# Key blocks of a decode attention dealt to the partitions in another order

One Trainium2 chip, one core. The metric is the device time of one execution in microseconds (us); lower is better. Ratios between two kernels are the mean time of one kernel's fast runs over that of the other's fast runs of the same rounds, so they are not quite the ratio of the medians quoted beside them.

## The reference

One decode step: layer norm of 4 rows of 512, then attention over a cache and a small gated feed-forward in parallel, summed with x. What matters here is the size of the cache, 4 batches x 32 heads x 8192 keys x 128 in bf16, for K and for V:

```python
q = ((xn @ wq).reshape(B, 1, 32, 128)).transpose(0, 2, 1, 3)
scores = einsum("bhqd,bhkd->bhqk", q, k_cache) * 128 ** -0.5
p = softmax(scores)                          # over 8192 keys
o = einsum("bhqk,bhkd->bhqd", p, v_cache)    # any order of keys gives the same sum
return x + o.transpose(...).reshape(B, 1, 4096) @ wo + swiglu_ffn(xn)
```

That is 256 blocks (128 of K, 128 of V) of 2 MiB, each read once: 536.9 MB of the 550.8 MB that the kernel reads.

## The kernel before

Each (head, batch) pair is one step. Its K block goes to one of nine slots of 128 partitions x 16 KiB, V four steps behind. The row of a partition is 64 keys in a row in HBM, 16 KiB. DVE, the vector engine, transposes K; PE, the matrix engine, makes scores and, for V, the weighted sum. Partitions are the 128 rows of SBUF, the memory on the chip; HBM is the large memory beside it. The profile shows 16 DMA engines that carry data between the two in packets: 33330 of the 42210 packets are of 8 KB or more, here mostly one row of 16 KiB each.

```python
T = Sk // P                # 64 keys for each partition
SLOT = T * Dh              # 8192 bf16 = 16 KiB for each partition
NSLOT = 9
...
def load_k(m):
    h, b = divmod(m, B)
    t_ = slot()
    nc.sync.dma_start(out=t_[:], in_=A_k_cache[b, h, :, :].rearrange("(p t) d -> p (t d)", p=P))
    k_tiles[m] = t_

def load_v(m, parts=1):
    h, b = divmod(m, B)
    t_ = slot()
    src = A_v_cache[b, h, :, :].rearrange("(p t) d -> p (t d)", p=P)
    w = SLOT // parts
    for i in range(parts):
        nc.sync.dma_start(out=t_[:, i * w:(i + 1) * w], in_=src[:, i * w:(i + 1) * w])
    v_tiles[m] = t_
...   # (cut: layer norm, q projection, feed-forward, softmax, output projection)
for i in range(M + LP + 1):          # M = 128 steps, LP = 4
    if i + 2 < M:
        load_k(i + 2)
    if 0 <= i + 2 - LP < M:
        load_v(i + 2 - LP, parts=4 if i + 2 - LP == M - 1 else 1)
    ...   # output weights are loaded at steps 115 and 116 as rows of 1 KiB
```

## Time and profile before

| | before |
|---|---|
| median of 4 runs | 1310.61 us (1310.52 to 1310.66) |
| DMA rate over the span | 421 GB/s |
| DMA engines busy | 99.5% of the span |
| PE / DVE busy | 1089.7 / 693.8 us |

The DMA engines bound the kernel; the prediction shows the lines. Two more lines of the page are needed for comparison. The first is the rate of the DMA in 40 equal slices of the span, the second the transfers of K (count, size, median us from issue to landing):

```profile
GB/s 393 429 425 428 426 427 428 427 427 426 427 429 426 426 428 426 427 428 425 429 426 428 426 427 427 427 426 427 428 428 426 425 429 426 427 394 412 425 428 288
slot<-in_A_k_cache_dram SPq DMA_DIRECT2D x128, 2048.0 KB, 39.0
```

The rate is flat at about 427 GB/s; the dip to 394 is where the output weights pass.

### The profile page before, as it was taken

The numbers are of one execution on the slowest core, as the hardware profiler recorded it, in microseconds if no ns is written. First come the engines' busy times: TensorE is split into PE (matmuls) and PEld (weight loads), VectorE is DVE, ScalarE is ACT, GpSimd is POOL, SyncE is SP. The second block draws the span as 40 slices with busy tenths as digits, with TensorE's granted clock in tenths as the row PEclk, the third lists the DMA queues.
The fourth block names the chain that finished last, engine by engine and source line by source line (L and its number), as shares of the span: only waits on it lengthen the run. The fifth ranks groups of instructions, "written<-read, shape, count | busy, mean of one in ns | idle before, by whom it ended". The sixth has DMA issues, their size and how long they took to land.

```text
span 1308.9 us, 11179 instructions
## 1 busy us (share of the span) xinstructions
PE 1089.7 (83%) x4610; PEld 423.3 (32%) x4676; DVE 693.8 (53%) x887; ACT 48.6 (4%) x102; POOL 5.6 (0%) x11
## 2 busy tenths in 40 slices
PE   5888888888888888888888888888988888886887
PEld 2243333333333333333333333333333333332333
DVE  7634554554554564554565555455555555544542
ACT  1000000000000000000000000000000000000000
POOL 1000000000000000000000000000000000000000
PEclk8889999999999999999999899999999999997999
DMA  9999999999999999999999999999999999999996
GB/s 393 429 425 428 426 427 428 427 427 426 427 429 426 426 428 426 427 428 425 429 426 428 426 427 427 427 426 427 428 428 426 425 429 426 427 394 412 425 428 288
DMA packets 42210, 551.49 MB, mean 421 GB/s; under 512 B 4264, under 2 KB 8368, under 8 KB 8880
## 3 DMA queue, kind: packets, MB, share of 16 engines
q1 hardware_dynamic: 42160, 550.79, 99.5%
q8 instruction: 36, 0.59, 0.2%
q14 instruction: 14, 0.11, 0.0%
HBM read 550.77 MB, written 0.00 MB: 421 GB/s over the span
## 4 chain that ended last, share of the span: by engine, by line
DMA 91%; PE 5%; DVE 3%; issue 0%; SPq 0%; ACT 0%; DVEq 0%; ACTq 0%
DMA slot<-in_A_k_cache_dram 86%; DMA slot<-in_B_w_up_dram 3%; DMA slot<-in_A_v_cache_dram 3%; DVE kt L252 2%; PE oacc L72 2%; PE sps L72 2%; PE xps L72 0%; SPq L93 0%; PE mps L274 0%; SPq L85 0%; DVE mx L268 0%; DVE res L384 0%; DVE zq L243 0%; PE mps L72 0%; ACT o_sb L309 0%
## 5 line engine op out<-in xcount | busy, mean ns | idle before, releaser
L252 DVE STREAM_TRANSPOSE kt<-slot 128x1024 uint32<-128x1024 uint32 x512 | 593.6, 1212 | 300.1 <-DMA slot<-in_A_k_cache_dram 295.4
L72 PE MATMUL sps<-kt,zq 128*128 128x512 bf16 x1982 | 566.9, 415 | 196.7 <-DVE kt L252 176.4
L72 PEld LDWEIGHTS <-zq 128*128 128x128 bf16 x2048 | 208.9, 103 | 544.4 <-issue 375.9
L298 DVE RECIPROCAL rcp<-mps 128x4 f32<-128x4 f32 x32 | 5.8, 182 | 162.5 <-PE mps L72 162.5
L268 DVE TENSOR_REDUCE mx<-sps 128x1 f32<-128x512 f32 x32 | 22.1, 691 | 40.5 <-PE sps L72 40.5
L277 DVE TENSOR_REDUCE nm<-mps 128x4 f32<-128x64 f32 x32 | 7.2, 224 | 50.2 <-PE mps L274 50.2
L72 PE MATMUL xps<-ident_f,o_sb 128*128 128x4 f32 x256 | 33.1, 253 | 0.7 <-ACT o_sb L309 0.7
L72 PEld LDWEIGHTS xps<-ident_f,o_sb 128*128 128x128 f32 x256 | 31.1, 192 | 1.2 <-ACT o_sb L309 1.2
L243 DVE COPY zq<-qt 32x16 bf16<-32x16 bf16 x128 | 23.5, 183 | 1.3
L318 DVE TENSOR_TENSOR otn<-xps,rcp 128x4 bf16<-128x4 f32 x32 | 5.2, 162 | 34.3 <-PE xps L72 34.3
L309 ACT COPY o_sb<-oacc 128x512 f32<-128x512 f32 x32 | 18.8, 586 | 20.8 <-PE oacc L72 20.7
L72 PE MATMUL oacc<-slot,pt__5656 128*4 128x512 bf16 x64 | 14.6, 379 | 0.1
L72 PE MATMUL oacc<-slot,pt__4008 128*4 128x512 bf16 x64 | 14.6, 379 | 0.1
L72 PE MATMUL oacc<-slot,pt__367 128*4 128x512 bf16 x64 | 14.6, 379 | 0.0
L72 PE MATMUL oacc<-slot,pt__918 128*4 128x512 bf16 x64 | 14.6, 379 | 0.0
L72 PE MATMUL oacc<-slot,pt__2154 128*4 128x512 bf16 x64 | 14.6, 379 | 0.0
L72 PE MATMUL oacc<-slot,pt__3802 128*4 128x512 bf16 x64 | 14.6, 379 | 0.0
L72 PE MATMUL oacc<-slot,pt__1330 128*4 128x512 bf16 x64 | 14.6, 379 | 0.0
L72 PE MATMUL oacc<-slot,pt__5862 128*4 128x512 bf16 x64 | 14.6, 379 | 0.0
L72 PE MATMUL oacc<-slot,pt__6719 128*4 128x512 bf16 x64 | 14.6, 379 | 0.0
L72 PE MATMUL oacc<-slot,pt__1536 128*4 128x512 bf16 x64 | 14.6, 379 | 0.0
L72 PE MATMUL oacc<-slot,pt__1742 128*4 128x512 bf16 x64 | 14.6, 379 | 0.0
(204 smaller groups left out, 636.5 us busy)
## 6 DMA issues: line engine op xcount, KB each, us to landing
slot<-in_A_k_cache_dram SPq DMA_DIRECT2D x128, 2048.0 KB, 39.0
slot<-in_A_v_cache_dram SPq DMA_DIRECT2D x127, 2048.0 KB, 39.2
slot<-in_A_wq_dram SPq DMA_DIRECT2D x2, 2048.0 KB, 9.6
slot<-in_A_wo_dram SPq DMA_DIRECT2D x2, 2048.0 KB, 29.8
slot<-in_A_v_cache_dram SPq DMA_DIRECT2D x4, 512.0 KB, 28.3
slot<-in_B_w_gate_dram SPq DMA_DIRECT2D x1, 1792.0 KB, 38.5
slot<-in_B_w_up_dram SPq DMA_DIRECT2D x1, 1792.0 KB
slot<-in_B_w_down_dram SPq DMA_DIRECT2D x1, 1792.0 KB, 33.2
```

The lines of the kernel that those rows point to most:

```text
L72: nc.tensor.matmul(out_ap, lhsT=lhsT, rhs=rhs, start=start, stop=True, skip_group_check=True, **kw)
L243: nc.vector.tensor_copy(out=zq[h % 2][a * QB:(a + 1) * QB, :, :, XO + a * QB].rearrange("p b (j r) -> p r j b", r=2), in_=qt[a * QB:(a + 1 ...
L252: nc.vector.transpose(out=kt[:].bitcast(dt.uint32).rearrange("p (j t r) -> p t j r", j=2, r=QB), in_=src.rearrange("p (t j r) -> p t j r", ...
L268: nc.vector.reduce_max(out=mx[:], in_=s_ps[h][:], axis=AX.X)
L277: nc.vector.tensor_reduce(out=nm[:], in_=mps[:, 0:P].rearrange("p (a x g r) -> p x a g r", a=NQ, x=B, r=2)[:, :, :, :, 0], axis=AX.XY, op= ...
L298: nc.vector.reciprocal(out=r_[:], in_=mps[:, P:P + B])
L309: nc.scalar.copy(out=o_sb[:], in_=o_acc[h % 2][:])
L318: nc.vector.tensor_tensor(out=otn[:, h, :], in0=xps[:], in1=rcp.pop(h)[:], op=ALU.mult)
```

## The change

Intent: let the 16 DMA engines read rows at the same time that are neighbours in HBM. The source becomes 16 x 8 rows: partition 8e+j takes key block 16j+e instead of block 8e+j. K and V change alike, so the result is the same. (The diff also adds an empty line, so line numbers after it are higher by one.)

```diff
     def load_k(m):
         h, b = divmod(m, B)
         t_ = slot()
-        nc.sync.dma_start(out=t_[:], in_=A_k_cache[b, h, :, :].rearrange("(p t) d -> p (t d)", p=P))
+        nc.sync.dma_start(out=t_[:], in_=A_k_cache[b, h, :, :].rearrange("(j e t) d -> e j (t d)", e=16, t=T))
         k_tiles[m] = t_
 
     def load_v(m, parts=1):
         ...
-        src = A_v_cache[b, h, :, :].rearrange("(p t) d -> p (t d)", p=P)
+        src = A_v_cache[b, h, :, :].rearrange("(j e t) d -> e j (t d)", e=16, t=T)
         w = SLOT // parts
         for i in range(parts):
-            nc.sync.dma_start(out=t_[:, i * w:(i + 1) * w], in_=src[:, i * w:(i + 1) * w])
+            nc.sync.dma_start(out=t_[:, i * w:(i + 1) * w], in_=src[:, :, i * w:(i + 1) * w])
```

## The prediction

> **What bounds the kernel now.** I read the views in this order: the slices of the page (is one resource full from end to end?), the windows (is the rate the same in every stage?), the chain that ended last (is that resource what sets the end?), and the waits (would another engine take over?).
>
> The slices show one row that never leaves 9 until the last slice, and it is DMA:
>
> ```profile
> PE   5888888888888888888888888888988888886887
> DVE  7634554554554564554565555455555555544542
> DMA  9999999999999999999999999999999999999996
> DMA packets 42210, 551.49 MB, mean 421 GB/s; under 512 B 4264, under 2 KB 8368, under 8 KB 8880
> q1 hardware_dynamic: 42160, 550.79, 99.5%
> ```
>
> The reader is to see that the 16 DMA engines together are busy 99.5% of the span, and that nearly all packets are large: 42210 - 8880 = 33330 of them are 8 KB or more. A 16 KiB packet is what one partition's row (T = 64 keys of 128 bf16) makes, so the large packets are the K and V rows: 256 blocks of 2 MiB, which is 536.9 of the 551.5 MB.
>
> The windows (columns: us of the stretch, busy time and count by engine, clock, DMA share, GB/s) show no stages in the long middle:
>
> ```profile
> 100.00:300.00 200.00, 169.31 (x707) 65.87 (x716) 107.39 (x138) 6.83 (x15) 0.00 (x0) 0.97 1.01 427
> 300.00:600.00 300.00, 252.48 (x1033) 97.02 (x1049) 162.21 (x205) 9.45 (x21) 0.00 (x0) 0.96 1.01 427
> 600.00:900.00 300.00, 254.18 (x1048) 98.01 (x1062) 159.92 (x204) 10.92 (x24) 0.00 (x0) 0.96 1.01 427
> ```
>
> 427 GB/s in each. The chain of waits (start us, us, what) is a string of K landings:
>
> ```profile
> 82.31 38.55 DMA slot<-in_A_k_cache_dram
> ...
> 120.92 39.16 DMA slot<-in_A_k_cache_dram
> ...
> 160.16 39.35 DMA slot<-in_A_k_cache_dram
> ...
> 199.58 39.15 DMA slot<-in_A_k_cache_dram
> ...
> 238.80 39.17 DMA slot<-in_A_k_cache_dram
> ```
>
> One link is 39.16 us: about eight transfers in the queue (nine slots, one being read), so 39.16 / 8 = 4.90 us for 2 MiB = 2.097 MB, or 428 GB/s. The same rate comes out of three views. The waits confirm that compute follows the data and not the reverse:
>
> ```profile
> DVE kt L252 <- DMA slot<-in_A_k_cache_dram: 295.4, 90, 10.5
> ```
>
> DVE, whose 512 transposes are the first use of K, sits 295 us for landings; PE is busy 1089.7 us by the page, 219 us short of the span. So the time is the bytes over the rate of the 16 engines, plus a few us at the ends, and only a change of that rate matters.
>
> [...]
> [...]
> [...]
> [...]
> [...]
>
> **The change part by part.** It removes nothing and adds nothing: 255 whole transfers of 2 MiB plus one V block in four quarters, the same bytes, rows of 16 KiB, tiles, DVE and PE work. K and V take the same permutation of key blocks, and softmax with its sum doesn't care about the order, so the result stays. What moves:
>
> (a) *HBM addresses of one step.* [...] On 536.9 MB / 427 GB/s = 1257 us of K and V[...] I expect 0 to 5 us, since a rate that equal in all stretches doesn't look like engines held up by memory.
>
> (b) *Who writes which partition.* The source's slowest dimension was 128 and becomes 16; the destination's remains 128. [...]
>
> [...] I choose 1.7. K and V: 1257 x 1.7 = 2137 us. The rest (head, tail, weights) is 1310.6 - 1257 = 53 us and unchanged. Sum 2190 us. In that time all compute is hidden: the busiest engine needs 1090 us.
>
> **Rivals.**
> *Same mapping, or ports no bound.* [...] the rate stays near 427. [...] Time 1300 to 1325 us; chance about 0.2.
> *HBM locality pays as intended.* [...]
> *Fewer engines.* If the new shape ran on 8 engines, K and V would take 2 x 1257 and the whole 2570 us. [...] It would look like lock-step in time; the DMA share tells them apart.
>
> **Range and chances.** In step throughout: 1257 x 2 + 53 = 2567 us; even spread: 1257 x 1.5 + 53 = 1939 us; mostly apart (ratio 1.11): 1450 us. I give 0.78 to the port collision, 0.20 to no change of note, 0.02 to a gain over 2%. The range 1450 to 2600 us holds the first alone, at about 8 in 10; the middle value is 2190.
>
> **What would show it.** Right: GB/s in the middle slices falls evenly from 427 to some 210 to 290, the DMA share stays near 9 (packets take longer; none is missing), packet count and bytes stay, K's landing goes from 39.0 to some 65 us, and DVE's wait for K grows by nearly all of the added time. PE and DVE busy times stay. A DMA share of about half with 16 KiB packets as quick as before would mean fewer engines. Middle slices at 425 to 430 mean that the mapping, or the port, isn't what I take it for; over 432 means that HBM order counted.

Passages are cut from the texts, here and before the experiments; the cuts are marked. The forecast came to 2190 us: 1257 x 1.7 = 2137 us for K and V and 53 us for the rest. An assumption, not shown before the experiments: with 16 x 8 rows the engines meet in pairs in the partitions that they write, and two that meet get half of the rate each. A pair that always meets ("in step") has the ratio 2.0, one that meets for half of its bytes ("even spread", of the leads of one engine over the other) 1.5, one that mostly does not 1.11; 1.7 was chosen between these. "Port" is only the name of this assumption.

## The result, and the profile after

| | before | after |
|---|---|---|
| median of 4 runs | 1310.61 us | 1948.78 us |
| lowest to highest | 1310.52 to 1310.66 | 1902.96 to 2011.77 |
| ratio of fast runs | | 1.4606 (95%: 1.4459 to 1.4754) |
| PE / DVE busy | 1089.7 / 693.8 us | 1247.8 / 696.0 us |

The kernel is correct and 46% slower by its fast runs (the medians of all four runs give 1948.78 / 1310.61 = 1.49). Its runs scatter by over 5%, while before they agree within 0.02%; two of the four, 1971.87 and 2011.77 us, count as slow because they are over 1.5% above the fastest. Their granted clocks (0.832 and 0.824, against 0.843 and 0.834) hardly set them apart, so this looks like scatter of the changed kernel itself rather than a state of the chip. The profile is of the one at 1971.87 us. So absolute times of its stages are those of a somewhat slow run; the reading below uses rates that differ by factors.

The page after: DMA share and rate by slice, packets, the DMA queue, and the transfers of K.

```profile
DMA  9999999999999999999999999999999999899997
GB/s 249 214 269 217 219 221 227 235 234 231 226 229 231 232 241 252 276 294 299 317 329 329 332 341 373 369 375 377 359 378 389 374 359 384 199 207 214 216 214 164
DMA packets 42210, 551.49 MB, mean 280 GB/s; under 512 B 4264, under 2 KB 8368, under 8 KB 8880
q1 hardware_dynamic: 42160, 550.79, 99.4%
slot<-in_A_k_cache_dram SPq DMA_DIRECT2D x128, 2048.0 KB, 52.8
```

Packets, bytes and sizes are those of before to the last digit, and the engines are as busy (99.4% against 99.5%). No work was added: each packet takes longer. In the two traces the median 16 KiB packet took 0.61 us before (300 to 900 us of the span) and 1.27 us after (15 to 115 us). The GB/s row is the finding. In slices 2 to 6 it is 214 to 221, half of before, apart from 269 in the third: there the feed-forward weights pass in their old order, and from 130 to 140 us, when nearly only they land, the window shows 413 GB/s, against 216 from 110 to 120 us and 213 from 145 to 150 us. So the old order runs at nearly full speed and the new one at half within 40 us of each other. From slice 7 on the row climbs slowly, to 359 to 389 in slices 25 to 34, and falls back to 199 to 216 in the next five (164 in the last, where the work runs out).

The windows of the kernel after (us of the stretch, busy time and count by engine, clock, DMA share, GB/s) give the numbers of these three stages:

```profile
15.00:115.00 100.00, 53.06 (x200) 19.21 (x193) 39.52 (x49) 3.99 (x5) 0.00 (x0) 0.83 1.01 215
1560.00:1660.00 100.00, 76.22 (x300) 28.84 (x300) 44.67 (x56) 2.73 (x6) 0.00 (x0) 0.91 1.01 370
1710.00:1900.00 190.00, 93.14 (x330) 33.62 (x329) 42.65 (x54) 2.73 (x6) 0.00 (x0) 0.74 1.00 212
```

At a DMA share of 1.0 throughout, the rate is 427 / 215 = 1.99 times lower than before in the first stage. The waits say who pays (us in total, times, longest):

```profile
DVE kt L253 <- DMA slot<-in_A_k_cache_dram: 828.3, 117, 25.1
PE oacc L72 <- DMA slot<-in_A_v_cache_dram: 124.9, 63, 5.8
```

DVE waits 828.3 - 295.4 = 533 us longer for K, of the 661 us by which the span grew; PE now waits for V too, for which it waited 0.5 us before. PE's busy time grew although its matmuls are the same: its clock was granted at 0.832 against 0.952, and the mean score matmul took 500 ns against 415 (also, 66 of the 2048 score matmuls are missing from the trace before, an estimated 19 us at the mean of the recorded ones). It is still far from the span.

The fall near the end comes where the output weights are loaded. Just before and during it (issues on the DMA queue: start, us):

```profile
1662.28 0.40 SPq L233 DMA_DIRECT2D slot<-in_A_wo_dram  x1
1667.78 42.41 SPq L94 DMA_DIRECT2D slot<-in_A_k_cache_dram  x1
1710.28 0.55 SPq L103 DMA_DIRECT2D slot<-in_A_v_cache_dram  x1
```

The K transfer behind the weights needs 42.41 us to be issued instead of 0.54 (29.47 instead of 0.33 in the kernel before, where the rate fell no lower than 364), and meanwhile the engines run out of work:

```profile
1700.00:1710.00 10.00, 4.80 (x12) 1.71 (x12) 4.62 (x4) 0.00 (x0) 0.00 (x0) 0.52 0.41 102
```

A DMA share of 0.41 means that the engines had work for less than half of the time. After it the rate is that of the kernel's beginning. My first reading was that all engines start again at the same time; experiment 4 tests it.

### The profile page after: what moved, and what is told of

It reads as the page before. It is cut to its first block, busy times and chain, and to the rows that moved or that the text cites. A ratio compares the mean times of both kernels' runs of the same rounds, so it can differ in the third digit from the quotient of the medians.

```text
span 1970.1 us, 11245 instructions
## 1 busy us (share of the span) xinstructions
PE 1247.8 (63%) x4676; PEld 468.9 (24%) x4676; DVE 696.0 (35%) x887; ACT 48.6 (2%) x102; POOL 5.6 (0%) x11
## 3 DMA queue, kind: packets, MB, share of 16 engines
q1 hardware_dynamic: 42160, 550.79, 99.4%
## 4 chain that ended last, share of the span: by engine, by line
another core or an unknown queue 34%; DMA 33%; PE 19%; DVE 12%; issue 2%; SPq 0%; DVEq 0%; ACT 0%; ACTq 0%
DMA slot<-in_A_v_cache_dram 30%; DVE kt L253 10%; PE sps L72 10%; PE oacc L72 7%; DMA slot<-in_A_k_cache_dram 3%; PE mps L72 1%; PE xps L72 1%; DVE zq L244 1%; SPq L94 0%; PE mps L275 0%; DVE nm L278 0%; DVE otn L319 0%; DVE nm L280 0%; DVE nb L282 0%
## 5 line engine op out<-in xcount | busy, mean ns | idle before, releaser
L72 PE MATMUL sps<-kt,zq 128*128 128x512 bf16 x2048 | 692.2, 500 | 574.8 <-DVE kt L253 570.3
L253 DVE STREAM_TRANSPOSE kt<-slot 128x1024 uint32<-128x1024 uint32 x512 | 594.1, 1213 | 828.3 <-DMA slot<-in_A_k_cache_dram 828.3
L72 PEld LDWEIGHTS <-zq 128*128 128x128 bf16 x2048 | 244.7, 120 | 1013.5 <-issue 916.1
L72 PE MATMUL oacc<-slot,pt__712 128*4 128x512 bf16 x64 | 19.6, 473 | 10.6 <-DMA slot<-in_A_v_cache_dram 10.6
L72 PE MATMUL oacc<-slot,pt__6494 128*4 128x512 bf16 x64 | 19.3, 467 | 10.0 <-DMA slot<-in_A_v_cache_dram 10.0
L72 PE MATMUL oacc<-slot,pt__6719 128*4 128x512 bf16 x64 | 18.0, 442 | 11.3 <-DMA slot<-in_A_v_cache_dram 11.3
L72 PE MATMUL oacc<-slot,pt__6909 128*4 128x512 bf16 x64 | 17.9, 461 | 10.4 <-DMA slot<-in_A_v_cache_dram 10.4
L72 PE MATMUL oacc<-slot,pt__367 128*4 128x512 bf16 x64 | 16.3, 410 | 9.4 <-DMA slot<-in_A_v_cache_dram 9.4
L72 PE MATMUL oacc<-slot,pt__1742 128*4 128x512 bf16 x64 | 16.3, 410 | 8.3 <-DMA slot<-in_A_v_cache_dram 8.3
L72 PE MATMUL oacc<-slot,pt__2154 128*4 128x512 bf16 x64 | 16.0, 403 | 8.6 <-DMA slot<-in_A_v_cache_dram 8.6
L72 PE MATMUL oacc<-slot,pt__1536 128*4 128x512 bf16 x64 | 16.3, 409 | 7.8 <-DMA slot<-in_A_v_cache_dram 7.8
L72 PE MATMUL oacc<-slot,pt__918 128*4 128x512 bf16 x64 | 14.6, 379 | 10.0 <-DMA slot<-in_A_v_cache_dram 10.0
L72 PE MATMUL oacc<-slot,pt__1948 128*4 128x512 bf16 x64 | 16.3, 410 | 7.1 <-DMA slot<-in_A_v_cache_dram 7.1
L72 PE MATMUL oacc<-slot,pt__1330 128*4 128x512 bf16 x64 | 14.6, 379 | 9.4 <-DMA slot<-in_A_v_cache_dram 9.4
L72 PE MATMUL oacc<-slot,pt__1124 128*4 128x512 bf16 x64 | 14.6, 379 | 7.5 <-DMA slot<-in_A_v_cache_dram 7.5
## 6 DMA issues: line engine op xcount, KB each, us to landing
slot<-in_A_k_cache_dram SPq DMA_DIRECT2D x128, 2048.0 KB, 52.8
```

The source lines that it names most:

```text
L72: nc.tensor.matmul(out_ap, lhsT=lhsT, rhs=rhs, start=start, stop=True, skip_group_check=True, **kw)
L253: nc.vector.transpose(out=kt[:].bitcast(dt.uint32).rearrange("p (j t r) -> p t j r", j=2, r=QB), in_=src.rearrange("p (t j r) -> p t j r", ...
```

## The experiments

The theory from the prediction, an assumption to be tested: the new source shape makes another cut of the transfer over the engines, so that two engines meet in the partitions that they write and slow each other (the "port theory"). The rivals: reading neighbours in HBM is what costs; the new shape costs in itself (descriptors, fewer engines). Experiments 1 to 4 ran on one chip, 5 to 8 on a second, 9 and 10 together and 11 alone, each group with its own runs of the kernel before. Experiments 8, 10 and 11 are single executions of state unknown; their readings are factors of about two within one execution.

**1. Another shape of the source: 64 x 2 rows.**

```diff
-  ...rearrange("(j e t) d -> e j (t d)", e=16, t=T)     # both K and V
+  ...rearrange("(j e t) d -> e j (t d)", e=64, t=T)
```

> Source as 64 x 2 rows instead of 16 x 8 (correct result): key block j*64+e goes to partition 2e+j. [...] the slowest dimension of the source is again not that of the destination[...]. Port theory: slow like the changed kernel, 1850 to 2100 us, first slices at about 215 GB/s. Theory that HBM neighbours are what costs: 1305 to 1330 us, 427 GB/s.

Measured: 1310.64 us, ratio 1.0001 (0.9986 to 1.0016), correct. My expectation missed entirely. A shape unlike the destination's is not what costs, nor a permuted order of keys. Which shapes keep the rate and which do not became the question; experiment 5 asks it.

**2. Rows nearer in HBM, with the old shape.**

```diff
+    def near(c, b, h):
+        a = c[b, h, :, :]
+        return bass.AP(a.tensor, a.offset, [[2048, P], [1, SLOT]])   # rows 4 KiB apart
-    in_=A_k_cache[b, h, :, :].rearrange("(p t) d -> p (t d)", p=P)   # both K and V
+    in_=near(A_k_cache, b, h)
```

> The source keeps 128 rows as slowest dimension, but they start 4 KiB apart and overlap (wrong result on purpose)[...]; partitions, packets and bytes moved are those of before. Port theory: within 1% of before, 1297 to 1320 us, 425 to 433 GB/s. Theory that neighbours in HBM cost: about 1950 us, 215 to 380 GB/s.

Measured: 1310.47 us, ratio 0.9999 (0.9984 to 1.0014). Rows that are nearer to each other in HBM, 4 KiB instead of 16 KiB from one to the next, alone neither gain nor cost. (This kernel, and those of experiments 4, 6 and 7, passed the comparison with the reference although their keys are wrong. The comparison doesn't see such an error here, so a pass isn't evidence that an order of keys is right; the orders of the change and of 1 and 5 are right by construction.)

**3. A small lead for some of the engines.** By the assumption two engines that meet would not do so if one were far enough ahead; transfers of 4 and 12 rows were to put some of the engines ahead of others. Which engines carry them is not shown.

```diff
+    def lead():
+        rows = A_k_cache[0, 0, :, :].rearrange("(p t) d -> p (t d)", p=P)
+        nc.sync.dma_start(out=head[64:68, :], in_=rows[64:68, :])    # 4 rows
+        nc.sync.dma_start(out=head[0:12, :], in_=rows[0:12, :])      # 12 rows
+    lead()
     load_k(0)                      # after.py otherwise; once more behind the output weights
```

> The changed kernel with two small transfers ahead of the first K block and again behind the second half of the output weights: 4 rows[...] and 12 rows[...]. [...] Port theory:[...] first slices at 340 to 427 GB/s instead of 215, slices after the output weights likewise, 1330 to 1650 us. Theory of HBM order, of descriptors or of fewer engines: no change, 1900 to 2010 us, first slices at 215 GB/s.

Measured: 2106.45 us (2091.90 to 2224.88), a loss and no gain (ratio 1.6073 against 1.4606): the climb begins later. The rate by slice:

```profile
GB/s 239 217 263 219 221 222 223 223 221 222 221 221 220 221 222 223 227 247 249 248 250 273 246 270 328 368 364 349 371 364 389 386 357 361 292 183 219 226 224 180
```

A miss, and it left two readings: leads don't count, or the lead wasn't what I meant. Each row of the small transfers is one packet of 16 KiB, while an engine's share of a whole transfer, if the 16 share it evenly, is 128 / 16 = 8 packets, an estimate; half a share would be four. In the trace every 16 KiB packet that started in the first microsecond of this stage took from 0.88 to 2.4 us, against 0.61 right before; of the first sixteen none was quick. So, if these were on sixteen engines, those without a small transfer slowed down too. That gave a new theory, which experiments 10 and 11 test: where any pair meets, all engines are held up, and not the two of the pair alone ("any pair" below, against "each pair for itself").

**4. The output weights as large packets.**

```diff
-    in_=A_wo[...].rearrange("(h p) e -> p h e", p=P)     # 16 rows of 1 KiB for each partition
+    in_=A_wo[...].rearrange("(p h) e -> p h e", p=P)     # one row of 16 KiB
```

> The changed kernel with the output weights loaded as rows of 16 KiB per partition instead of 16 rows of 1 KiB (wrong result on purpose). If the fall to 207 GB/s near the end comes from the queue running dry behind the 4096 small packets[...], then it is gone: the last slices stay above 330 GB/s and the time falls by 100 to 170 us, to 1770 to 1880 us. If it has another cause (which heads, the end of the kernel), the last slices stay near 210 GB/s and the time at 1900 to 2010 us.

Measured: 1926.45 us (1885.12 to 2075.94), no clear gain over 1948.78 (ratio 1.4492, 1.4367 to 1.4616, against 1.4606). The median lies in the range that I gave for "another cause"; the slices lie between both branches. The rates of the run of 1885.12:

```profile
GB/s 254 220 275 219 220 220 220 222 222 223 227 228 231 236 236 243 284 300 306 313 314 326 342 365 378 380 381 374 379 364 374 377 387 370 368 272 234 277 331 222
```

After the weights it is 272, 234, 277, 331 instead of 199 to 216, so the fall recovers, but it is not gone. The trace of this run settles one thing: the queue never ran dry. The K transfer behind the first weights was issued in 0.55 us, and from 1680 to 1720 us the DMA share is 1.00 and the rate still 218 to 220 GB/s. So this fall to half speed came without an empty queue, and the empty queue is not shown to be its cause in the changed kernel either. What both kernels have in common there is that transfers in the old order pass among those in the new; whether these shift the engines against each other was not tested. The scatter of 10% between runs of this kernel forbids to say more on the time.

**5. 32 x 4 rows: runs of 4 partitions for each index.**

```diff
-  ...rearrange("(j e t) d -> e j (t d)", e=16, t=T)     # both K and V
+  ...rearrange("(j e t) d -> e j (t d)", e=32, t=T)
```

> Source as 32 x 4 rows (correct result): key block j*32+e goes to partition 4e+j. [...] 64 x 2 ran at the speed of before, so equality of the slowest dimensions is not the condition;[...] Port theory with that rule: 1305 to 1316 us, 427 GB/s. Theory that rows in HBM one behind the other collide: over 1500 us.

Measured: 1310.57 us against 1310.50, ratio 1.0000 (0.9988 to 1.0013), correct. Its rate by slice is that of before:

```profile
GB/s 392 430 425 426 428 426 427 426 429 426 427 427 427 427 426 428 424 430 427 426 428 426 429 425 427 426 427 429 425 427 428 426 426 428 425 394 412 428 426 292
```

The step from 32 x 4 to 16 x 8 is the whole loss. (Only 128, 64 x 2, 32 x 4 and 16 x 8 were tried: a rule by the partitions in a row for each index, 8 against 4 and fewer, and one by the size of the slowest dimension, 16 against 32 and more, fit them alike.) It is also the best version of the idea that I found, and it gains nothing.

**6. 16 x 8 rows at other addresses.**

```diff
+    def far(c, b, h):
+        a = c[b, h, :, :]
+        return bass.AP(a.tensor, a.offset, [[4 * SLOT, 16], [SLOT, 8], [1, SLOT]])
-    in_=A_k_cache[b, h, :, :].rearrange("(j e t) d -> e j (t d)", e=16, t=T)   # both K and V
+    in_=far(A_k_cache, b, h)
```

> The changed kernel with 16 x 8 rows of another place (wrong result on purpose):[...] only the shape of the source is the changed kernel's. Port theory: 1850 to 2100 us, first slices at 213 to 220 GB/s. Theory of HBM order: 1305 to 1330 us, 427 GB/s.

Measured: 2028.63 us (1997.71 to 2081.32), ratio 1.5347. The rate by slice (of the run at 2032.46 us):

```profile
GB/s 248 216 263 220 220 225 241 242 237 235 235 243 245 242 241 245 244 286 274 248 233 268 292 321 355 374 376 385 385 364 374 388 361 358 140 206 218 218 218 177
```

It starts at 216 to 225 GB/s (263 with the feed-forward weights), as in the changed kernel. The 5% between 1.5347 and 1.4606 is about the scatter of either (5.7% and 4.2% between lowest and highest). With experiment 2 this settles the first rival: rows 4 KiB apart in the old shape are fast (1310.47 us), and 16 x 8 rows are slow at two sets of addresses, here with 16 KiB between the 8 rows of an index and in the change with 256 KiB.

**7. Only K in the new order.**

```diff
 # after.py, but in load_v:
-        src = A_v_cache[b, h, :, :].rearrange("(j e t) d -> e j (t d)", e=16, t=T)
+        src = A_v_cache[b, h, :, :].rearrange("(p t) d -> p (t d)", p=P)
```

> Only K takes the new order, V keeps the old one (wrong result on purpose). Half of the bytes are concerned. Port theory: if the pairs stay in step in the K transfers,[...] the whole 1257/2 * 2 + 1257/2 + 53 = 1939 us; with a lead spread evenly 1257/2 * 1.5 + 1257/2 + 53 = 1624 us; so 1600 to 1940 us, about 285 GB/s in the first slices. A cost that needs K and V both would leave less than 1400 us.

Measured: 2434.85 us, ratio 1.8515, far outside of the 1600 to 1940 us expected. Half of the change costs 1.8 times as much extra time as the whole: (2434.85 - 1310.5) / (1948.78 - 1310.6). The windows:

```profile
30.00:130.00 100.00, 61.51 (x270) 25.31 (x273) 36.92 (x46) 2.14 (x5) 0.00 (x0) 0.76 1.01 278
400.00:2000.00 1600.00, 871.92 (x2936) 323.57 (x2979) 454.52 (x575) 28.51 (x63) 0.00 (x0) 0.79 1.00 228
```

It starts at 278, near the 285 that I had worked out for pairs in step in K and none in V. Then it falls to 228 and stays. The V transfers, in the old order, are slow as well: V takes 73.6 us from issue to landing and K 74.1, against 39.2 and 39.0 before. Over the span that is 550.8 MB / 2436.4 us = 226 GB/s, against 280 with both in the new order and 421 with both in the old. Why two orders in one queue were slower than either is not shown; the reading is that they let engines meet that never do within one order.

**8. Transfers alone, by stage.** No compute; each stage 56 MiB of transfers into seven slots, drained between stages.

```python
stage(rows(P), P, 28)                # (1) 128 rows in order
stage(rows(P, 2), P, 28)             # (2) 128 rows, each 32 KiB from the next
stage(cut(16), P, 28)                # (3) as changed
stage(cut(32), P, 28)                # (4) as in experiment 5
stage(rows(64), 64, 56)              # (5) 64 partitions only
stage(rows(16), 16, 112)             # (6) 16 partitions only
stage(cut(16), P, 28, lead)          # (7) as changed, behind two small transfers
```

> Transfers alone, no compute (wrong result on purpose), seven stages of 56 MiB, drained between them. Port theory, GB/s in the steady part: (1) 128 rows as before 427; (2) 128 rows 32 KiB apart[...], 427; (3) 16 x 8 rows as changed 213 to 220; (4) 32 x 4 rows 427; (5) 64 partitions alone[...], 213 and never more; (6) 16 partitions[...], 107; (7) 16 x 8 again, behind two small transfers[...]: 340 to 427 if leads decide, 213 to 220 if they don't. HBM theory: (2) or (4) slower than 420, (5) and (6) not bound at 213 and 107.

Measured in windows inside each stage (the last two columns are DMA share and GB/s):

```profile
40.00:140.00 100.00, 0.00 (x0) 0.00 (x0) 1.00 1.01 429
180.00:280.00 100.00, 0.00 (x0) 0.00 (x0) 1.00 1.01 429
320.00:540.00 220.00, 0.00 (x0) 0.00 (x0) 1.00 1.01 218
580.00:680.00 100.00, 0.00 (x0) 0.00 (x0) 1.00 1.01 430
720.00:960.00 240.00, 0.00 (x0) 0.00 (x0) 1.00 1.01 205
1000.00:1240.00 240.00, 0.00 (x0) 0.00 (x0) 1.00 1.01 109
1300.00:1500.00 200.00, 0.00 (x0) 0.00 (x0) 1.00 1.01 220
```

Stages 1 to 6 came out within 5% of what was expected. The fifth and sixth show that the partitions written can cost by themselves: transfers to 64 of the partitions get 205 GB/s, to 16 neighbouring ones 109, about a half and a quarter of 429, with the engines busy all the time; the changed order gets 218, the half. No compute is needed for the loss. Stage 7 missed: again no gain from a lead. Its main transfers came to the queue only after the small ones had begun, and each small transfer was one packet a row, so the lead was not four packets; the next run mends that.

**9. A lead of four packets in the kernel.**

```diff
+    def lead(n=4):
+        rows = A_k_cache[0, 0, :, :].rearrange("(p t) d -> p (t d)", p=P)
+        for i in range(n):
+            nc.sync.dma_start(out=head[96 + 4 * i:100 + 4 * i, :], in_=rows[0:4, :])
+        for i in range(n):
+            nc.sync.dma_start(out=head[12 * i:12 * i + 12, :], in_=rows[0:12, :])
+    lead()
     load_k(0)                      # after.py otherwise; once more two steps behind the output weights
```

> The changed kernel (correct result) with eight small transfers ahead of the first K block and again a little after the output weights: four of 4 rows[...] and four of 12 rows[...]. [...] New theory[...]: first slices 400 to 427 GB/s, 1320 to 1450 us. Old theory (each pair for itself, leads give 1.0 to 2.0): the same here. If leads don't count: 1900 to 2110 us, first slices 215 GB/s.

Measured: 1784.29 us (1705.58 to 1896.32), correct. Only one of the four runs counts as fast, so no ratio is given. It is the only variant of 16 x 8 with a median below 1900 us, but far from the 1320 to 1450 expected. The rates of the run of 1787.85 us:

```profile
GB/s 233 257 269 270 284 308 299 293 284 301 296 274 285 326 388 358 356 373 382 356 367 378 368 356 379 382 378 356 381 383 356 337 370 217 203 175 213 215 212 178
```

Eight small transfers of 1 MiB in all lift slices 2 to 14 from 214 to 235 GB/s, as the changed kernel has them, to 257 to 326 (the third slice holds other weights in both). After the output weights, the second set doesn't help.

**10. Doses of the lead, transfers alone.** Four stages of 42 transfers of 16 x 8; after 14 of each, the lead of experiment 9 with n = 2, 4, 6, 8. The lead of 8 packets is a control: by the estimate of 8 packets for each engine it would put the engines a whole transfer apart, in step again. A fifth stage has 16 partitions 7 apart.

> Transfers alone (wrong result on purpose). Four stages of 42 transfers of 16 x 8 rows; after 14 of each a lead of 2, 4, 6 and 8 packets is put in. Every stage begins at 218 GB/s. After the lead: any-pair theory 218, 427, 218, 218; each pair for itself 285, 427, 285, 218; leads don't count 218 in all. Fifth stage: 16 partitions 7 apart[...]. GB/s must be 213 either way[...]. Each pair for itself:[...] DMA share about 0.6. Any-pair theory: all packets slow, share about 1.

Measured, after the lead in each stage, then the fifth stage:

```profile
180.00:380.00 200.00, 0.00 (x0) 0.00 (x0) 1.00 1.01 222
600.00:760.00 160.00, 0.00 (x0) 0.00 (x0) 1.00 1.01 280
980.00:1180.00 200.00, 0.00 (x0) 0.00 (x0) 1.00 1.01 220
1420.00:1620.00 200.00, 0.00 (x0) 0.00 (x0) 1.00 1.01 219
1700.00:1960.00 260.00, 0.00 (x0) 0.00 (x0) 1.00 1.01 211
```

Before the lead the four stages ran at 213, 214, 216 and 212. Only the dose of four helps clearly: 222, 280, 220, 219. If each pair went for itself, 2 and 6 were to give 285 by the expectation. They give almost nothing, as the any-pair theory expected. The same shape ran at 214 GB/s before the dose of four and at 280 after it, so the shape as such does not set the rate; that the relative place of the engines does is the reading, since the lead itself was not measured. Nor were engines lost, since the changed kernel itself reached 389 GB/s, where half of the engines at the 427 / 16 = 26.7 each of before would carry 214. The size was missed: 280, not 427, and it stays open. In the fifth stage the DMA share is 1.01 while the rate, 211, is the half: no engine sits idle while others are slow. All are held up.

**11. One partition exchanged.**

```python
for first in (11, 4, 0, 11):          # 16 rows of 16 KiB to 16 partitions
    stage(rows(16), slice(first, first + 106, 7), 280)
```

> Transfers alone (wrong result on purpose), 280 in each of four stages, every one 16 rows of 16 KiB to 16 partitions 7 apart[...]. [...] Stages: start at 11, 4, 0, 11.[...] 427, then less, less, 427 GB/s. Any-pair theory: one pair costs as much as two, 205 to 215 GB/s at a DMA share of 1.0. Each pair for itself: also 213 GB/s[...], share about 0.55. Proportional loss: one pair 400 GB/s, two 375.

(By the assumption no engines meet with the start at 11, one pair with the start at 4, two with the start at 0. No run shows that.)

Measured in windows inside each stage, in this order:

```profile
60.00:200.00 140.00, 0.00 (x0) 0.00 (x0) 1.00 1.00 383
260.00:540.00 280.00, 0.00 (x0) 0.00 (x0) 1.00 0.78 217
600.00:880.00 280.00, 0.00 (x0) 0.00 (x0) 1.00 1.01 211
940.00:1080.00 140.00, 0.00 (x0) 0.00 (x0) 1.00 1.00 382
```

Shifting the same 16 rows by 7 partitions takes the rate from 383 to 217 GB/s; of the partitions written, 4 takes the place of 116 and the other fifteen stay. So the exchange of one partition in sixteen decides. Partition 4 is not slow by itself, since transfers to all 128 ran at 429 (experiment 8); which of the other fifteen it may share something with, this run does not show. (That it is 383 and not 427 may come from transfers of 256 KiB in 16 packets; this was not tested.) The exchange costs 383 - 217 = 166 GB/s, the start at 0 only 6 more. The share of 0.78 with the start at 4 is between both theories (1.0 and 0.55): packets are slowed, but the engines also run out of work; with the start at 0 (1.01) they do not. The packets in the trace say the same: the median 16 KiB packet took 0.61 us with the start at 11, 0.97 at 4 and 1.24 at 0, where engines that merely waited for two others would still show 0.61. "Any pair slows all" is thus too strong for the start at 4 and fits the start at 0.

## Why the prediction was right, and where its steps were not

- *What bounds the kernel.* Right. The engines are busy as before and the time follows the rate; compute stayed hidden.
- *(a) HBM addresses: 0 to 5 us.* Right: with 128 rows in order, 4 KiB from one to the next took 1310.47 us (experiment 2), 16 KiB ran at 427 to 429 GB/s (before; experiment 8, first stage) and 32 KiB at 429 (second stage); the 32 x 4 order gave 427 to 430 (experiments 5, 8).
- *(b) The cut.* What is shown: the loss goes with 16 x 8 and not with addresses (experiments 2, 5, 6), it needs no compute (8: 218 GB/s), the rate depends on which partitions are written (8 and 11: 64 partitions 205, 16 neighbours 109, 16 that lie 7 apart 383, and 217 with one of these exchanged), and small transfers put in between can relieve it (10: from 214 to 280). The trace names no engines, so which engine takes which partition, what engines share, and their meeting in pairs inside the changed kernel remain assumptions, which these runs fit but do not show. I applied the assumption wrongly once: a source unlike the destination isn't enough (experiment 1, 1310.64 us).
- *The size, 1.7.* Too large. (1948.8 - 53) / 1257 = 1.51, the value the prediction gave for an even spread of leads, but not for that reason. The rate is not 1.51 times lower throughout: it is 1.99 times lower at the start and 427 / 212 = 2.01 at the end, and 427 / 370 = 1.15 times late in the middle. The mean of 1.5 is a mean over a drift. So the direction and the lower bound of the rate were foreseen; where in its wide range (ratios 1.11 to 2.03) the time would fall was not, and that it fell near the value for an even spread is chance.
- *One ratio from start to end; each pair for itself.* This step failed twice. In these runs pairs, if there are any, are not for themselves: with one partition of sixteen exchanged the median packet took 0.97 us instead of 0.61 (11), and in the fifth stage of 10 all engines are busy (1.01) at half of the rate. And the rate climbs without any lead put in, from 214 to 389 GB/s over more than 1000 us, so, if the places of the engines set it, something moves them toward a good place. What moves them stays open; that it comes out differently in each run is the likely source of the 5% scatter, which is argued and not shown.
- *What would show it.* The 210 to 290 GB/s "evenly" in the middle slices was wrong for the second half (up to 389). K's time to landing was predicted too long, some 65 us where 52.8 were measured (39.0 before), for the same reason. PE busy time did not stay: 1247.8 us against 1089.7, at the lower clock. The rest held: share near 9, equal packets and bytes, DVE busy time, and DVE's wait for K larger by most of the added time (533 of 661 us).

## What to carry to other kernels

When the DMA engines are already busy for 99.5% of the span at a flat 427 GB/s, the question about a new order of addresses is what else the access pattern changes: the addresses alone gained nothing here (1310.47 us in experiment 2, 1310.57 in 5, against 1310.5). Here the shape of the DRAM side decided where the rate began; that it does so by deciding which engine writes which partition is the assumption: 32 x 4 rows kept 427 GB/s and 16 x 8 halved it, with the same bytes, packets and share of busy engines. So read the GB/s row beside the busy row, since engines that hold each other up look fully busy (a share of 1.01 at 215 GB/s); and where a source must be split over 128 partitions, try runs of at most four partitions for each index of its slowest dimension: 1, 2 and 4 ran as before here (1310.6 us) and 8 did not (1948.78 us); other shapes were not tried.
